# First weight batch of a spectral-mixing kernel: raw loads on GpSimd's queue, conversions in rounds

## The chip, the cores and the metric

The kernel runs on one core of a Trainium2 chip. The metric is the device time of one execution in microseconds (us), and each version is judged by the median of its runs. Engines are named as the profile names them: PE (TensorE), DVE (VectorE), ACT (ScalarE), POOL (GpSimd), and SP, the engine that issues most of the transfers. A transfer is issued on the queue of an engine and is carried by 16 DMA engines that all queues share.

## The reference

The reference filters a signal in the frequency domain along the sequence and passes the result through a two-layer block:

```python
# x: (8, 3008, 256) f32, filt_r, filt_i: (1505, 256) f32, w_in: (256, 2048) f64, w_out: (2048, 256) f64
X = np.fft.rfft(x, axis=1)
Y = X * (filt_r + 1j * filt_i)[None]
y = np.fft.irfft(Y, n=3008, axis=1).astype(np.float32).reshape(8 * 3008, 256)
h = y @ w_in
out = ((h - np.tanh(h)) @ w_out).astype(np.float32)
```

The weights come as 64-bit floats, which no engine computes with, so the kernel loads them as raw 64-bit words and builds 32-bit floats from their bits.

## The kernel before

**The transform.** The length 3008 is split as 64 x 47. For each batch there is a first stage (a matmul with `wf1` over the 64 points, whose results are stored to DRAM as `ct1`), a middle stage (read back as `a2`, one matmul with a matrix from `fg`, the product with the filter, a second pair of matmuls with `fg` and its turned copy `gx`, stored to DRAM as `ct2`), and a last stage (read back as `e2`, matmuls with `s2`, results in `ut`). Batches are worked off in units: batch 0 alone, then three pairs, then batch 7 alone.

**The two-layer block.** For every group of rows `up` makes h with Strassen-like products of `wu`, `shrink` computes h - tanh(h), and `down` multiplies with `wd`. `wu` and `wd` have seven strips: some come straight from the weights, the others are sums of strips, made on POOL by `sums`, four operations for each quarter of the columns. There are eight quarters: 0 to 3 for `wu`, 4 to 7 for `wd`. Both blocks run interleaved for all units, by an order that is written out by hand (`manual_schedule`): each engine executes its instructions in program order.

**The opening.** Before the interleaved loop begins, unit 0 goes through its first stage (`first0`, lines 853 to 876) and its 16 middle steps (the loop of line 966, j = 0 to 15, two steps to a group c of four matrices) with nothing beside them but the loading of weights. The change is confined to this opening.

- `converted` (line 191) handles one job, half a quarter: a 512 KB transfer into a tile `raw` (three buffers), three DVE operations that split the bits (lines 204 to 207), two operations for mantissa and exponent (ACT at lines 216 and 217, or DVE at 211 and 213 if `alone` is set), and four or five closing DVE operations (lines 219 to 230), the first of which reads `raw` for the last time.
- `weights_alone` (line 293) converts quarters 0 to 2 (six jobs) wholly on DVE during and after the first stage. `weights` (line 270) converts quarters 3 to 5 (six jobs), a round at each middle step. Both load `raw` on SP's queue. Quarters 6 and 7 follow in the main loop (`weights_slow`).
- At each even step the filters of the group after next are fetched by `filters_of` (line 878): six transfers on POOL's queue (ten for the last group). At each odd step `double_filters` (line 888, two ACT copies) prepares the filters of the next group and `turned` (line 895, two POOL operations) makes its `gx`.
- A middle step issues the loads for later groups on SP (`load_a2`, line 378; `load_slots`, line 370), the matmuls `pz`, then `back0` for the step before (line 951: matmuls `pe`, ACT copy to `e1s`, store to `ct2`), then the two filter products on DVE (lines 983 and 984), and then the weight round. "The gap" below is the time between the last middle step and the first matmuls `pu` of the last stage: the last store of `ct2` must land and be read back as `e2`.

Of the kernel before, what the change touches and what calls it, by code (L numbers as in the profile page):

```python
# [143 lines left out]
def kernel(  # L144
# [9 lines left out]
    nc = tc.nc  # L154
    V, G, ACT = nc.vector, nc.gpsimd, nc.scalar
# [35 lines left out]
    def converted(tiles, src, dsts, queue, alone=False):  # L191

        n = src.shape[-1] * (src.shape[1] if len(src.shape) == 3 else 1)
        t = tiles("raw", I64, n)
        queue.dma_start(t if len(src.shape) == 2 else
                        t.rearrange("p (h n) -> p h n", h=src.shape[1]), src)
        yield
        words = t.bitcast(I32).rearrange("p (n w) -> p n w", w=2)  # L200
        lo, hi = words[:, :, 0].bitcast(U32), words[:, :, 1]
        it, pt, st = (tiles(k, I32, n) for k in ("it", "pt", "st"))
        ft = tiles("ft", F32, n)
        V.tensor_scalar(out=it, in0=hi, scalar1=0xFFFFF, scalar2=None, op0=ALU.bitwise_and)
        V.tensor_scalar(out=pt, in0=hi, scalar1=20, scalar2=0x7FF,
                        op0=ALU.logical_shift_right, op1=ALU.bitwise_and)
        V.tensor_scalar(out=st, in0=hi, scalar1=-2 ** 31, scalar2=None, op0=ALU.bitwise_and)
        yield

        if alone:  # L210
            V.tensor_scalar(out=ft, in0=it, scalar1=2.0 ** -20, scalar2=1.0,
                            op0=ALU.mult, op1=ALU.add)
            V.tensor_scalar(out=pt, in0=pt, scalar1=-896.0, scalar2=0.0,
                            op0=ALU.add, op1=ALU.max)
        else:
            ACT.activation(ft, it, AF.Identity, bias=1.0, scale=2.0 ** -20)
            ACT.activation(pt, pt, AF.Relu, bias=exp_b)
        yield
        V.scalar_tensor_tensor(out=ft, in0=lo, scalar=2.0 ** -52, in1=ft,
                               op0=ALU.mult, op1=ALU.add)  # L220
        V.tensor_scalar_min(pt, pt, 255.0)
        yield
        V.scalar_tensor_tensor(out=pt, in0=pt, scalar=23, in1=st,
                               op0=ALU.logical_shift_left, op1=ALU.bitwise_or)
        pt = pt.bitcast(F32)
        for cols, dst, sign in dsts:
            f, p = ft[:, cols], pt[:, cols]
            if len(dst.shape) == 3:
                f, p = (v.rearrange("p (h n) -> p h n", h=dst.shape[1]) for v in (f, p))
            V.scalar_tensor_tensor(out=dst, in0=f, scalar=sign, in1=p, op0=ALU.mult, op1=ALU.mult)  # L230
        yield

    def parts_of(quarters):

        jobs = []
        for k in quarters:
            u = k % 4
            for h in range(2):
                if k < 4:
                    cols = slice(256 * u, 256 * u + 256)  # L240
                    src = bass.AP(tensor=moe_w_in.tensor, offset=128 * h * DFF + 256 * u,
                                  ap=[[DFF, 128], [DFF // 2, 2], [1, 256]])
# [12 lines left out]
        return jobs  # L255
# [6 lines left out]
        G.tensor_sub(w[:, 2], w[:, 1], w[:, 5])  # L262
        G.tensor_sub(w[:, 6], w[:, 0], w[:, 6])

    def begun(tiles, job, alone=False):
        j = converted(tiles, *job, nc.sync, alone)
        next(j)
        return j

    def weights(tiles, quarters, ahead):  # L270


        jobs = parts_of(quarters)
        began = [begun(tiles, job) for job in jobs[:ahead]]
        yield
        for k in range(len(jobs) + 1):
            if k < len(jobs):
                next(began[k])
            if k > 2 and k % 2:
                sums(quarters[k // 2 - 1])  # L280
            yield
            if k < len(jobs):
                next(began[k])
            if k > 0:
                for _ in began[k - 1]:
                    pass
            if k + ahead < len(jobs):
                began.append(begun(tiles, jobs[k + ahead]))
            yield
        sums(quarters[-1])  # L290
        yield

    def weights_alone(tiles, quarters):

        jobs = parts_of(quarters)
        began = [begun(tiles, job, True) for job in jobs[:2]]
        yield
        for k in range(len(jobs)):
            if k + 2 < len(jobs):
                began.append(begun(tiles, jobs[k + 2], True))  # L300
            for _ in began[k]:
                pass
            if k % 2:
                sums(quarters[k // 2])
            yield

    def weights_slow(tiles, quarters):

        jobs = parts_of(quarters)
        began = [begun(tiles, job) for job in jobs[:2]]  # L310
        yield
        for k in range(len(jobs)):
            for _ in began[k]:
                yield
            if k + 2 < len(jobs):
                began.append(begun(tiles, jobs[k + 2]))
            if k % 2:
                sums(quarters[k // 2])
                yield
# [511 lines left out]
    with tc.tile_pool(name="tr", bufs=2) as tr, tc.manual_schedule():  # L831
        with tc.tile_pool(name="pro", bufs=1) as pro, \
# [62 lines left out]
            def turned(g3, t):  # L895


                G.tensor_copy(t[0:RP], g3[IM:IM + RP])
                G.tensor_scalar_mul(t[IM:IM + RP], g3[0:RP], -1.0)
# [12 lines left out]
            V.memset(near_b, B)  # L912
            V.memset(exp_b, -896.0)
            xs = [load_x0(0, (0, 4, 8)), load_x0(1), load_x0(2)]
            ws = weights_alone(tiles0, range(3))

            pad = pro.tile([64, DM], F32, name="pad")
            G.memset(pad, 0.0)
# [12 lines left out]
            mats = {0: load_slots(0, pro)}  # L931
            next(ws)
            for c in range(3):
                for k, _ in enumerate(first0(xs[c], c)):
                    if k == 3:
                        next(ws)
            G.dma_start(s2, s2_d)
            turned(mats[0][1], gx[0])
            fts[1] = filters_of(1)
# [1 line left out]
            mats[1] = load_slots(1, pro)  # L941
            a2[1] = load_a2(0, 1, False, "ft")
            double_filters(fts[0], 0)
            for _ in ws:
                pass
            ws = weights(tiles0, range(3, 6), 2)
            next(ws)
            e1s = pro.tile([128, 4, 2, DM], F32, name="e1s")
            waiting = []

# [15 lines left out]
            for j in range(NK // 2):  # L966
                c = j // 2
                if j % 2 == 0 and c + 1 < NK // 4:
                    if c + 2 < NK // 4:
                        a2[c + 2] = load_a2(0, c + 2, False, ("a2", "ft")[c % 2])  # L970
                        mats[c + 2] = load_slots(c + 2, pro)
                        fts[c + 2] = filters_of(c + 2)
                pz = z0("pz", [128, 2, DM])
                for i in range(2):
                    k = (2 * j + i) % 4
                    nc.tensor.matmul(pz[:, i], mats[c][0][0:R2, k],
                                     a2[c][0:R2, k * DM:k * DM + DM], start=True, stop=True)
                if waiting:
                    back0()
                uv = tr.tile([128, 2, DM], F32, tag="uv", bufs=2, name="uv")  # L980
                zs = tr.tile([128, 2, DM], F32, tag="zs", bufs=2, name="zs")
                ft = fts[c][:, :, j % 2 * 2:j % 2 * 2 + 2]
                V.tensor_mul(uv, pz, ft[:, 0])
                V.tensor_mul(zs, pz, ft[:, 1])
                waiting.append((j, uv, zs))
                next(ws, None)
                if j % 2 and c + 1 < NK // 4:
                    double_filters(fts[c + 1], c + 1)
                    turned(mats[c + 1][1], gx[(c + 1) % 2])
                if j == NK // 2 - 3:  # L990
                    fs = first(1, z1)
                    next(fs)
                if j == NK // 2 - 1:
                    e2s[0] = load_e2(*groups[0], None, slice(0, 48))
            back0()
            for _ in range(EARLY):
                next(fs)
            load_e2(*groups[0], e2s[0], slice(48, 64))
            for _ in ws:
                pass  # L1000


        with tc.tile_pool(name="dn", bufs=2) as dn, \
# [40 lines left out]
            for U in range(total + 2):  # L1044
                i, u = divmod(U, 4)
                if U < total:
                    p, c = groups[i]
# [114 lines left out]
```

## Time and profile before

| what | value |
|---|---|
| median of 4 runs | 2839.16 us (2837.45 to 2841.6) |
| profiled execution, own time | 2838.55 us |
| its span, first to last instruction | 2836.7 us |
| mean granted PE clock | 0.988 |
| busy share of PE, DVE, ACT, POOL | 96%, 67%, 66%, 63% |
| first filter product of the middle stage (L983) | 52.51 us after the start |
| last filter product (L984) | starts at 112.36 us |
| first matmul of the last stage (L511) | 121.69 us |

The profile gives busy times, waits with the instruction or transfer that ended them, and stretches of the span. Times in it count from the start of the span. "L983" is line 983 of the kernel. A transfer's "issue" is the short time that it occupies its queue's engine; it lands later.

### The profile page before, as it was taken

Reading aid. Unit: us, or ns where it says so; the run is one execution under the profiler, and the core shown is the slowest. Engines: PE = TensorE matmul, PEld = TensorE weight load, DVE = VectorE, ACT = ScalarE, POOL = GpSimd, SP = SyncE. Lnnn points to the kernel's source line nnn. Section 1 sums busy time; section 2 is a strip of 40 time slices with the busy share of each in tenths; the row PEclk is TensorE's granted clock in tenths of the full one; section 3 lists DMA queues with packets and bytes.
Section 4 is the critical chain, followed back from the end, with each engine's and each line's share of the span. In section 5 each row is a group of like instructions: output and inputs, shape, how many; then the busy total and the mean of one; then the engine's idle time right before and its main releaser. Section 6 shows DMA issues by size and latency. Waiting matters only on the chain.

```text
span 2836.7 us, 36615 instructions
## 1 busy us (share of the span) xinstructions
PE 2728.6 (96%) x12418; PEld 2266.4 (80%) x12418; DVE 1913.9 (67%) x2170; ACT 1881.8 (66%) x2794; POOL 1793.4 (63%) x1407
## 2 busy tenths in 40 slices
PE   4799999999999999999999999999999999999998
PEld 2567777988877787888877787788888888898887
DVE  6565655666766677656666776676676767677776
ACT  2476766666767776666666667666676666666665
POOL 5456887544677767744577777755466667656555
PEclk7899999999999999999999999999999999999999
DMA  9754443232233332232332223212222322101010
GB/s 247 203 184 109 115 107 85 67 104 75 66 81 75 79 72 58 49 89 79 73 94 67 70 71 78 52 43 64 65 65 61 80 55 52 35 17 27 16 22 17
DMA packets 322592, 217.53 MB, mean 77 GB/s; under 512 B 224782, under 2 KB 274746, under 8 KB 322156
## 3 DMA queue, kind: packets, MB, share of 16 engines
q1 hardware_dynamic: 266826, 157.28, 23.7%
q10 hardware_dynamic: 52818, 51.53, 6.0%
q0 software_dynamic: 2752, 6.30, 0.8%
q8 instruction: 100, 1.64, 0.2%
q14 instruction: 96, 0.79, 0.1%
HBM read 138.87 MB, written 79.17 MB: 77 GB/s over the span
## 4 chain that ended last, share of the span: by engine, by line
PE 77%; ACT 9%; issue 5%; DVE 4%; DMA 3%; POOL 1%; ACTq 1%; DVEq 0%; SPq 0%; POOLq 0%
PE o L653 31%; PE x L545 20%; PE z L545 9%; PE y L545 5%; PE pe L411 3%; PE pu L511 3%; ACT y L601 3%; PE pz L430 3%; PE pf L351 2%; DVE h L607 1%; ACT u L551 1%; ACT zs L444 1%; ACT y L602 1%; DVE uv L445 1%; ACT zs L443 1%
## 5 line engine op out<-in xcount | busy, mean ns | idle before, releaser
L653 PE MATMUL o<-t,wd 128*128 128x256 f32 (+2 forms) x3072 | 774.8, 375 | 1.8 <-POOL t L526 1.3
L607 DVE TENSOR_TENSOR h<-h,y 128x1024 f32<-128x1024 f32 (+2 forms) x384 | 571.8, 1489 | 279.7 <-ACT y L602 279.7
L653 PEld LDWEIGHTS o<-t,wd 128*128 128x128 f32 x3072 | 579.3, 190 | 73.8 <-POOL t L526 1.6
L545 PE MATMUL x<-tu,wu 128*128 128x256 f32 (+2 forms) x2304 | 588.8, 378 | 15.4 <-ACT u L551 15.1
L653 PE MATMUL o<-h,wd 128*128 128x256 f32 (+2 forms) x2304 | 581.5, 375 | 0.2 <-DVE h L611 0.2
L611 DVE SCALAR_TENSOR_TENSOR h<-sq,h 128x1024 f32<-128x1024 f32 (+2 forms) x384 | 567.0, 1477 | 20.5 <-ACT y L601 0.5
L524 POOL TENSOR_TENSOR t<-h 128x512 f32<-128x512 f32 (+2 forms) x192 | 240.3, 1252 | 502.4 <-DVE h L611 444.7
L545 PEld LDWEIGHTS x<-tu,wu 128*128 128x128 f32 x2304 | 427.8, 190 | 159.1 <-issue 73.1
L653 PEld LDWEIGHTS o<-h,wd 128*128 128x128 f32 x2304 | 430.7, 190 | 71.2 <-issue 18.8
L608 ACT ACTIVATE sq<-y,near_b 128x1024 f32<-128x1024 f32 (+2 forms) x384 | 435.6, 1134 | 5.0 <-DVE h L611 0.2
L601 ACT ACTIVATE y<-h 128x1024 f32<-128x1024 f32 (+2 forms) x384 | 400.0, 1042 | 14.8 <-ACT e L414 8.0
L602 ACT ACTIVATE y<-y 128x1024 f32<-128x1024 f32 (+2 forms) x384 | 399.2, 1040 | 12.1
L551 ACT COPY s<-x 128x512 f32<-128x512 f32 (+2 forms) x192 | 110.9, 577 | 443.3 <-PE x L545 434.7
L527 POOL TENSOR_TENSOR t<-t,h 128x512 f32<-128x512 f32 (+2 forms) x192 | 307.6, 1602 | 0.1
L551 ACT COPY u<-x 128x512 f32<-128x512 f32 (+2 forms) x384 | 219.3, 571 | 55.5 <-PE x L545 20.0
L525 POOL TENSOR_TENSOR t<-h,t 128x512 f32<-128x512 f32 (+2 forms) x192 | 241.2, 1256 | 15.1
L526 POOL TENSOR_TENSOR t<-h 128x512 f32<-128x512 f32 (+2 forms) x191 | 248.1, 1299 | 0.0
L575 DVE TENSOR_TENSOR h<-z,u 128x512 f32<-128x512 f32 (+2 forms) x192 | 129.5, 675 | 171.3 <-ACT u L551 168.4
L446 POOL TENSOR_TENSOR zs<-zs,ft 128x512 f32<-128x512 f32 x112 | 166.0, 1483 | 101.9 <-ACT zs L444 101.8
L447 POOL TENSOR_TENSOR uv<-uv,zs 128x512 f32<-128x512 f32 x112 | 213.8, 1909 | 14.0 <-DVE uv L445 5.5
L545 PE MATMUL x<-ut,wu 128*128 128x256 f32 (+2 forms) x768 | 199.3, 382 | 4.8 <-DVE h L581 3.0
L561 DVE TENSOR_TENSOR h<-y,s 128x512 f32<-128x512 f32 (+2 forms) x192 | 130.4, 679 | 104.9 <-PE y L545 87.5
(119 smaller groups left out, 3384.7 us busy)
## 6 DMA issues: line engine op xcount, KB each, us to landing
a<-ct SPq DMA_DIRECT2D x64, 384.0 KB, 4.1
ft<-filt SPq DMA_DIRECT2D x96, 256.0 KB, 4.5
out_dram<-ot SPq DMA_DIRECT2D x1392, 16.0 KB, 1.5
ct<-e ACTq DMA_DIRECT2D x112, 192.0 KB, 2.6
ct<-a ACTq DMA_DIRECT2D x80, 256.0 KB, 2.9
x_sb<-in_x_dram SPq DMA_DIRECT2D x69, 256.0 KB, 2.8
e<-ct SPq DMA_DIRECT2D x33, 512.0 KB, 4.4
fg<-fg SPq DMA_DIRECT2D x40, 392.0 KB, 6.4
```

The lines of the kernel that those rows point to most:

```text
L524: G.tensor_sub(t[0], b[0][1], b[0][0])
L525: G.tensor_sub(t[1], b[1][1], t[0])
L526: (V if shared else G).tensor_sub(t[2], b[1][1], b[0][1])
L527: G.tensor_sub(t[3], t[1], b[1][0])
L545: nc.tensor.matmul(bank[:, k], wu[:, q - 1, (2 * u + k) * 128:(2 * u + k + 1) * 128], rhs[q - 1], start=(first and k == 0), stop=True, ski ...
L551: ACT.copy(t, X)
L601: ACT.activation(y[k], ht[k], AF.Arctan, scale=S)
L602: ACT.activation(y[k], y[k], AF.Square, accum_out=y_sums[:, 2 * U + k // 2:2 * U + k // 2 + 1])
L607: V.tensor_mul(ht[k], ht[k], y[k])
L608: ACT.activation(sq[k], y[k], AF.Square, bias=near_b, scale=A)
L611: V.scalar_tensor_tensor(out=ht[k], in0=sq[k], scalar=K, in1=ht[k], op0=ALU.add, op1=ALU.mult)
L653: nc.tensor.matmul(product(q), wd[:, q - 1, (2 * u + k) * 128: (2 * u + k + 1) * 128], rhs[q - 1][:, k], start=(u == 0 and k == 0 and q == ...
```

## The change

- `weights` takes over quarters 0 to 4 (ten jobs), in rounds, with its two middle operations on ACT. `weights_alone` is gone. Quarter 5 (two jobs) is a generator of its own.
- All twelve raw loads of the opening go to POOL's queue (`G`).
- Two raw loads are issued before the first stage, none within it. Behind the first stage come five rounds: all but the end of jobs 0 and 1, and the first three operations of job 2. Each middle step has one round, and at odd steps it now stands behind `double_filters` and `turned`. So jobs 2 to 9 fall into the middle steps (the end of job 9 behind them).
- The raw loads of quarter 5 are issued at step 13; its conversion and its sums stand in the gap, with those of quarter 4.

```diff
-    def weights(tiles, quarters, ahead):
+    def weights(tiles, quarters):
         jobs = parts_of(quarters)
-        began = [begun(tiles, job) for job in jobs[:ahead]]
+        began = [begun(tiles, job, G) for job in jobs[:2]]
         yield
         for k in range(len(jobs) + 1):
             if k < len(jobs):
                 next(began[k])
...
             if k > 0:
                 for _ in began[k - 1]:
                     pass
-            if k + ahead < len(jobs):
-                began.append(begun(tiles, jobs[k + ahead]))
+            if k + 2 < len(jobs):
+                began.append(begun(tiles, jobs[k + 2], G))
             yield
...
-    def weights_alone(tiles, quarters):
...
-            ws = weights_alone(tiles0, range(3))
+            ws = weights(tiles0, range(5))
...
             for c in range(3):
-                for k, _ in enumerate(first0(xs[c], c)):
-                    if k == 3:
-                        next(ws)
+                for _ in first0(xs[c], c):
+                    pass
...
             double_filters(fts[0], 0)
-            for _ in ws:
-                pass
-            ws = weights(tiles0, range(3, 6), 2)
-            next(ws)
+            for _ in range(5):
+                next(ws)
...
                 waiting.append((j, uv, zs))
-                next(ws, None)
                 if j % 2 and c + 1 < NK // 4:
                     double_filters(fts[c + 1], c + 1)
                     turned(mats[c + 1][1], gx[(c + 1) % 2])
+                next(ws)
                 if j == NK // 2 - 3:
                     fs = first(1, z1)
                     next(fs)
+                    ws_gap = weights(tiles0, range(5, 6))
+                    next(ws_gap)
...
             load_e2(*groups[0], e2s[0], slice(48, 64))
-            for _ in ws:
-                pass
+            for w in (ws, ws_gap):
+                for _ in w:
+                    pass
```

More of the change, by code (lines that the diff above doesn't have):

```diff
@@ L263, in sums, with begun @@
         G.tensor_sub(w[:, 6], w[:, 0], w[:, 6])
-    def begun(tiles, job, alone=False):
-        j = converted(tiles, *job, nc.sync, alone)
+    def begun(tiles, job, queue, alone=False):
+        j = converted(tiles, *job, queue, alone)
         next(j)
         return j
-    def weights(tiles, quarters, ahead):
+    def weights(tiles, quarters):
         jobs = parts_of(quarters)
-        began = [begun(tiles, job) for job in jobs[:ahead]]
+        began = [begun(tiles, job, G) for job in jobs[:2]]
         yield
@@ L291, in weights @@
         yield
-    def weights_alone(tiles, quarters):
[L295 to L301, printed above, removed]
-                pass
-            if k % 2:
-                sums(quarters[k // 2])
-            yield
     def weights_slow(tiles, quarters):
         jobs = parts_of(quarters)
-        began = [begun(tiles, job) for job in jobs[:2]]
+        began = [begun(tiles, job, nc.sync) for job in jobs[:2]]
         yield
@@ L315, in weights_slow @@
             if k + 2 < len(jobs):
-                began.append(begun(tiles, jobs[k + 2]))
+                began.append(begun(tiles, jobs[k + 2], nc.sync))
             if k % 2:
@@ L998 @@
             load_e2(*groups[0], e2s[0], slice(48, 64))
-            for _ in ws:
-                pass
+            for w in (ws, ws_gap):
+                for _ in w:
+                    pass
         with tc.tile_pool(name="dn", bufs=2) as dn, \
```

## The prediction, on record before the result

> **What bounds the kernel now.** The page first. Behind the first slice PE is busy nine tenths to the end, so a change to the opening is worth what the opening gets shorter; in the first four slices (71 us each) the DMA engines are fullest.
>
> ```profile
> PE   4799999999999999999999999999999999999998
> DMA  9754443232233332232332223212222322101010
> ```
>
> Second, the stages as windows: busy us (count) of PE, PEld, DVE, ACT, POOL, then granted clock, DMA share and GB/s.
>
> ```profile
> 0.00:37.60 37.60, 13.89 (x26) 4.92 (x26) 15.51 (x34) 10.12 (x16) 17.74 (x30) 0.85 0.92 262
> 37.60:52.50 14.90, 3.75 (x8) 2.52 (x8) 13.82 (x29) 0.00 (x0) 5.62 (x8) 0.50 0.99 258
> 52.50:109.80 57.30, 42.78 (x161) 29.84 (x162) 44.62 (x81) 27.72 (x38) 48.76 (x71) 0.87 0.88 212
> 109.80:121.70 11.90, 7.15 (x30) 4.54 (x28) 2.58 (x4) 4.11 (x7) 0.00 (x0) 1.00 0.55 154
> ```
>
> From 37.6 to 52.5 DVE is full and ACT idle: DVE converts weights while the first filter product waits. From 52.5 to 109.8 POOL is the fullest. Third, DVE's timeline at the seam, then POOL's near the end.
>
> ```profile
> 51.84 0.76 DVE L230 SCALAR_TENSOR_TENSOR wu<-conv 128x256 f32<-128x256 f32 x2
> 52.51 0.68 DVE L983 TENSOR_TENSOR uv<-pz,filt 128x512 f32<-128x512 f32 x1
> ```
> ```profile
> 84.15 0.76 POOL L885 DMA_DIRECT2D filt<-in_filt_r_dram  x1
> 84.90 0.55 POOL L885 DMA_DIRECT2D filt<-in_filt_i_dram  x1
> ...
> 89.71 0.60 POOL L885 DMA_DIRECT2D filt<-in_filt_r_dram  x1
> 90.30 0.55 POOL L885 DMA_DIRECT2D filt<-in_filt_i_dram  x1
> 93.13 0.56 POOL L885 DMA_DIRECT2D filt<-in_filt_r_dram  x1 [2.27 <-DMA filt<-in_filt_r_dram]
> 94.86 0.54 POOL L885 DMA_DIRECT2D filt<-in_filt_i_dram  x1 [1.17 <-DMA filt<-in_filt_i_dram]
> ...
> 99.16 0.72 POOL L260 TENSOR_TENSOR wd<-wd 128x256 f32<-128x256 f32 x1
> ...
> 103.67 1.24 POOL L899 TENSOR_SCALAR gx<-fg 48x384 f32<-48x384 f32 x1
> ```
>
> L983 starts the moment the conversions end. The issue at 93.13 is the eighth behind the one at 84.15 and waited for a landing, and so did 94.86 behind 84.90: I read that POOL's ninth transfer waits until the first has landed. The sums (99.16) stand ahead of the turned copy (103.67), for which PE waits until 104.96. From 52.68 to 109.79 POOL worked without a break but for such landings (6.4 us in five waits). So three things bound the opening: DVE at its start, POOL with its landings in its middle, DMA close behind both.
>
> **The first stage.** Five raw loads run beside it now; then three and the next group's filters: 2560 - 1536 - 376 = 648 KB less, at 262 GB/s 2.5 us. The bounds are 0 (the raw loads now stand in a third queue beside the stores) and 4 us; I take 2. The load of `a` (L382), issued at 37.64, goes at 35.6.
>
> **The first product.** PE's first pz began at 42.48, 4.84 behind that issue; its four matmuls take about 1.9, so the product could start at 44.4 and starts at 52.51: 8.1 us stand in DVE's queue. DVE then has only job 0, three operations each of jobs 1 and 2: 3.6 + 1.0 + 1.0 us (L204 to L230 without contention), beside the first stage's tail. First product: 42.4, 10 us earlier. If raw load 2 lands late, all of this is lost; it is issued near 26 and landings of raw loads took 9.8 us in the median, 16.2 at most, so the cover is real.
>
> **The middle steps.** Six jobs lay in them, now nearly eight, still one job to two steps, with their middle operations on ACT as before; a pair of steps costs DVE 2 x 1.2 + 3.6 = 6.0 us, ACT about 5.2. Raw loads 4 to 9 are issued here by POOL, so SP no longer holds `a` and `fg` behind them; that I cost at nothing, for PE waited for `a` once (9.5 us, at the start). POOL gains an issue of about 0.7 us per pair (its issues took 0.51 to 0.76). The raw issue waits for the job's L219 on DVE, and behind it on POOL stand `turned`, sums and filters. The walk, with 3.45 us for six filter issues, 1.75 for a turned copy, 3.2 for sums: raw 4 at 43.6 (product, then L219), turned and sums to 49.25, filters 3 to 52.7, raw and turned to 55.15. Filters 4 now meet the ninth-transfer rule: a raw load makes seven transfers per pair, so each waits for the one issued just one pair and one issue before. What a landing takes there is the disputed size. Filters landed in 6.7 us in the median and 10.0 at most from 50 to 110; with the raw loads ahead of them in their queue I take 8.0, and 0.3 to release. Then filters 4 go on at 57.55 and end at 60.4; with raw, turned and sums filters 5 start at 66.05, end at 69.5; filters 6 go on at 74.35, end at 77.2; sums to 82.85; filters 7 start at 83.15, their ninth at 91.45; raw 9 at 92.6; turned 6 ends at 95.05 (104.9 before: the sums no longer stand ahead of it). Raw 9 lands at 100.6, its three operations end at 101.6, and behind them on DVE waits the product of step 14 (110.08 before). From there to the end of the last pe took 5.0 us (115.06); the closing four operations of job 8, 2.55 us, now stand between the last two products, of which 0.3 is hidden: 7.25. The stage ends at 108.85, 6.2 us earlier. One us more of landing counts at four places (filters 4, 6, 7, raw 9) and costs 4 us.
>
> **The gap.** DVE gets the end of job 9 and jobs 10 and 11: 2.55 + 2 x 3.6 = 9.75 us, behind its last product; ACT their four operations (2.6 us), ahead of the `ut` copies; POOL two sums (6.4 us), ahead of the combination for `tu` (L524). By rows: the last sums end about 13 us behind the last pe, L524 and L525 1.4 later, and the matmul that reads `tu` stood 15 us behind it (130.01). So it is covered by half a us to a us; contention of DVE and POOL (L205 took 0.95 instead of 0.42 beside sums) may cost 0 to 4 us. I take 1. A raw load 11 landing over 6 us behind the last pe would stop ACT and so `ut`; it is issued 3 us before.
>
> **Sum.** -6.2 + 1 = -5.2 us on the profiled execution, whose own time was 2838.55 for a span of 2836.7 and lies 0.6 under the median: 2834.0 for the median. Nothing behind the opening changes place.
>
> **A rule against it.** From 37.6 to 52.5 the DMA engines were at 0.99 and 258 GB/s with the queues as they are. The Trainium skill, DMA: Bandwidth & Descriptors, Rules for kernel authors, says that spreading transfers over SP, ACT and GpSimd gains no bandwidth, as all run on the same engines. By it alone only the 2 us of the first stage and DVE's reordering would count, as here. The same page (Anatomy of one DMA) would give a 512 KB load 2.0 us plus size over 436 GB/s, 3.2 us as an estimate; the rows' 9.8 us contradict that under load, and by 3.2 us no landing would bind and the next case would follow.
>
> **Rivals.** (1) *The early start comes through.* Landings stay at the 6.7 us of now: 1.3 us less at four places ends the stage at 103.65, net -10.4, 2828.8. For it: SP's loads no longer wait for raw buffers, the DMA share from 52.5 to 109.8 is only 0.88. A floor is near: 14.5 MB between the load of `a` and raw 9 take 56 us at 258 GB/s, until 92. (2) *Slower: the ninth transfer.* Raw loads put 512 KB beside 376 KB of filters into one queue; if landings rise past 9.3 us, four waits eat the gain (114.1), and at 11 us the stage ends at 120.9, net +6.8, 2846. For it: landings up to 10.0, 16.2 for raw loads. Against: median 6.7. (3) *The move cancels*: POOL's chain, not DVE, sets the end at the same place, within 3 us of 2839; landings of 9 us do that.
>
> **How the numbers follow.** Forecast 0.40 (its own range 2830 to 2838: landings of 7 to 9 us, 4 us of time for each), rival 1 0.28, rival 2 0.20, rival 3 0.12. 0.2% is 5.7 us, about what a measurement can tell: faster than 2833.5 is rival 1 and less than half of the forecast (0.18), 0.46; slower than 2844.8 is rival 2, 0.20; between, 0.34. The range 2827 to 2846 leaves out the far ends.
>
> **What would show it.** L983 first at about 42; ACT copies (L216) for ten jobs before the gap; POOL waiting for raw and filter landings in the middle, 4 to 8 us in all; PE's pe ending near 109; `tu` (L524) within 2 us of its old distance. Wrong if L983 starts past 48, if DVE's L204 waits for raw loads by over 10 us, or if L524 waits for sums by over 3.

## The result, and the profile after

The changed kernel takes 2836.38 us in the median of 40 runs (2833.29 to 2839.31); the kernel before took 2839.95 in the median of 60 runs beside it (2834.83 to 2843.95). The ratio is 0.9987, 95% interval 0.9982 to 0.9991: 3.6 us faster, or 0.13%. The forecast was 2834.0, in the range 2827 to 2846. The profiled execution took 2835.7 us for a span of 2833.9; before it was 2838.55 for 2836.7.

Lines of `converted`, `sums` and `begun` (191 to 268) keep their numbers. Most lines behind `weights` stand 13 lower than before (`pu` L498, `ut` L500, `tu` L511 to L514, the filter loads L872, the doubled filters L876 and L877, the turned copies L885 and L886). From `back0` through the middle loop they stand 16 lower (the `pe` matmuls L941 and L943, the filter products L967 and L968).

The page's busy tenths, one digit for 71 us: a tenth more for PE in the first slice and nothing else for PE; the DMA engines differ by a tenth in three slices.

```profile
PE   5799999999999999999999999999999999999998
DMA  9754443233233322222332223212222322101010
```

The same four stages, and then the third one's first 47.5 us in two parts (busy us and count of PE, PEld, DVE, ACT, POOL; granted clock, DMA share, GB/s):

```profile
0.00:37.60 37.60, 14.52 (x26) 5.69 (x26) 5.02 (x14) 12.53 (x20) 20.85 (x35) 0.85 0.88 256
37.60:52.50 14.90, 11.79 (x41) 8.25 (x42) 11.35 (x21) 5.74 (x8) 11.29 (x17) 0.80 1.05 240
52.50:109.80 57.30, 42.93 (x157) 28.08 (x155) 46.02 (x86) 28.71 (x39) 42.71 (x63) 0.88 0.86 231
109.80:121.70 11.90, 4.95 (x19) 4.51 (x20) 10.06 (x20) 4.13 (x7) 5.91 (x8) 0.58 0.84 238
52.50:80.00 27.50, 19.70 (x76) 13.22 (x75) 19.72 (x38) 13.82 (x19) 20.32 (x31) 0.88 1.03 275
80.00:100.00 20.00, 14.17 (x52) 9.29 (x51) 17.40 (x31) 9.58 (x14) 19.08 (x28) 0.87 0.74 196
```

The second stage now does middle steps: ACT has 5.74 us of work there where it had none, PE 11.79 instead of 3.75. From 37.6 to 80 us the DMA engines are full, and from 80 to 100 POOL is busy for 19 of 20 us. The gap (109.8 to 121.7) holds 10 us of DVE's work instead of 2.6. DVE at the seam, then DVE and POOL near the end of the middle:

```profile
41.10 0.69 DVE L967 TENSOR_TENSOR uv<-pz,filt 128x512 f32<-128x512 f32 x1 [2.43 <-issue]
42.30 0.68 DVE L219 SCALAR_TENSOR_TENSOR conv<-raw,conv 128x512 f32<-128x512 uint32 x1
...
98.18 0.43 DVE L204 TENSOR_SCALAR conv<-raw 128x512 int32<-128x512 int32 x1 [2.46 <-DMA raw<-in_moe_w_out_dram]
...
100.73 0.69 DVE L967 TENSOR_TENSOR uv<-pz,filt 128x512 f32<-128x512 f32 x1 [0.39 <-ACT filt L876]
```
```profile
92.93 0.76 POOL L197 DMA_DIRECT2D raw<-in_moe_w_out_dram  x1
...
96.18 1.16 POOL L886 TENSOR_SCALAR gx<-fg 48x384 f32<-48x384 f32 x1
97.42 0.72 POOL L260 TENSOR_TENSOR wu<-wu 128x256 f32<-128x256 f32 x1
```

The first filter product starts at 41.10 instead of 52.51 and stands ahead of L219. The turned copy (96.18) is now ahead of the sums (97.42). The raw load of 92.93 holds DVE until 98.18, and the product of step 14 follows at 100.73 (110.08 before). The last `pe` ends at 107.80 instead of 115.22.

Marks of all kernels, from their traces, in us from the span's start. "Closing" is the start of the last of the 384 closing products of `shrink` (L598; L611 before); "main loop" is the way from `x<-tu`, the first matmul of `up` that reads `tu`, to it.

| kernel | `a` issued | first product | last `pe` ends | first `ut` copy | `x<-tu` | closing | main loop | span | median |
|---|---|---|---|---|---|---|---|---|---|
| before | 37.64 | 52.51 | 115.22 | 123.46 | 130.01 | 2816.79 | 2686.8 | 2836.7 | 2839.95 |
| before, second profile | 37.85 | 52.48 | 115.96 | 124.48 | 131.21 | 2818.10 | 2686.9 | 2837.8 | |
| after | 34.89 | 41.10 | 107.80 | 118.16 | 123.89 | 2812.80 | 2688.9 | 2833.9 | 2836.38 |
| after, second profile | 34.89 | 41.07 | 107.61 | 117.97 | 123.93 | 2813.26 | 2689.3 | 2832.9 | 2836.00 |
| SP's queue | 35.09 | 45.02 | 106.27 | 116.62 | 122.38 | 2810.11 | 2687.7 | 2831.5 | 2833.28 |
| old place | 34.94 | 41.22 | 106.06 | 116.42 | 122.91 | 2812.22 | 2689.3 | 2833.7 | 2835.58 |
| both of these | 33.81 | 43.85 | 106.96 | 117.32 | 123.68 | 2813.10 | 2689.4 | 2834.9 | 2836.99 |
| no gap | 34.97 | 41.21 | 107.41 | 115.77 | 121.39 | 2815.95 | 2694.6 | 2837.6 | 2839.69 |
| queue alone | 36.37 | 57.18 | 121.49 | 129.84 | 135.48 | 2823.45 | 2688.0 | 2845.3 | 2849.76 |
| one slot load | 35.56 | 41.64 | 102.25 | 112.61 | 118.59 | 2805.99 | 2687.4 | 2829.1 | 2832.07 |
| filters on SP | 40.10 | 46.35 | 116.26 | 126.61 | 133.47 | 2823.36 | 2689.9 | 2844.7 | 2844.85 |
| sums behind | 35.62 | 45.63 | 108.17 | 118.53 | 125.49 | 2814.91 | 2689.4 | 2837.1 | 2837.48 |
| gap in other tiles | 35.26 | 45.25 | 106.62 | 115.13 | 121.85 | 2811.59 | 2689.7 | 2833.4 | 2833.16 |
| delay | 35.86 | 42.22 | 108.99 | 119.35 | 128.49 | 2818.40 | 2689.9 | 2839.2 | 2839.29 |

### The profile page after: what moved, and what is told of

The parts are those of the page before. It is cut to its first block, busy times and chain, and to the rows that moved or that the text cites. A ratio compares the mean times of both kernels' runs of the same rounds, so it can differ in the third digit from the quotient of the medians.

```text
span 2833.9 us, 36616 instructions
## 1 busy us (share of the span) xinstructions
PE 2732.0 (96%) x12418; PEld 2272.7 (80%) x12418; DVE 1907.5 (67%) x2158; ACT 1889.0 (67%) x2806; POOL 1801.8 (64%) x1419
## 4 chain that ended last, share of the span: by engine, by line
PE 77%; ACT 9%; issue 5%; DVE 4%; DMA 2%; POOL 2%; ACTq 1%; SPq 0%; DVEq 0%; POOLq 0%
PE o L640 31%; PE x L532 20%; PE z L532 9%; PE y L532 5%; PE pe L398 3%; PE pu L498 3%; ACT y L588 3%; PE pz L417 3%; PE pf L338 2%; DVE h L594 1%; ACT u L538 1%; ACT zs L431 1%; ACT y L589 1%; DVE uv L432 1%; ACT zs L430 1%
## 5 line engine op out<-in xcount | busy, mean ns | idle before, releaser
L598 DVE SCALAR_TENSOR_TENSOR h<-sq,h 128x1024 f32<-128x1024 f32 (+2 forms) x384 | 566.7, 1476 | 20.8 <-DVE h L594 0.5
L511 POOL TENSOR_TENSOR t<-h 128x512 f32<-128x512 f32 (+2 forms) x192 | 240.4, 1252 | 500.2 <-DVE h L598 448.5
L514 POOL TENSOR_TENSOR t<-t,h 128x512 f32<-128x512 f32 (+2 forms) x192 | 307.0, 1599 | 0.1
L512 POOL TENSOR_TENSOR t<-h,t 128x512 f32<-128x512 f32 (+2 forms) x192 | 241.1, 1256 | 15.1
```

The lines of the kernel that those rows point to most:

```text
L511: G.tensor_sub(t[0], b[0][1], b[0][0])
L512: G.tensor_sub(t[1], b[1][1], t[0])
L514: G.tensor_sub(t[3], t[1], b[1][0])
L598: V.scalar_tensor_tensor(out=ht[k], in0=sq[k], scalar=K, in1=ht[k], op0=ALU.add, op1=ALU.mult)
```

## The experiments

Two questions: which part of the change brings the gain, and why 7.4 us at the last `pe` are 3.6 at the end. Each ratio is to runs of the kernel before taken beside the experiment (medians of 2838.71 to 2839.59 us).

**1. The raw loads back on SP's queue.** In the changed kernel:

```diff
-        began = [begun(tiles, job, G) for job in jobs[:2]]
+        began = [begun(tiles, job, nc.sync) for job in jobs[:2]]
...
-                began.append(begun(tiles, jobs[k + 2], G))
+                began.append(begun(tiles, jobs[k + 2], nc.sync))
```

> The changed kernel with its raw loads back on SP's queue; rounds, order and gap stay. Theory A (the gain is the reordering of the conversions; the queue is incidental): first filter product within 1 us of 41.1, last pe within 2 us of 107.8, median within 1.5 us of the changed kernel. Theory B (the gain is the queue: SP no longer holds the loads of a and fg behind raw buffers): last pe back at 112 to 115, median within 1 us of the kernel before.

2833.28 us, ratio 0.9982 (0.9973 to 0.9991). The first product comes 4 us later, as DVE waits 5.9 us for a raw load ahead of it, and the last `pe` 1.5 us earlier than in the changed kernel. Theory A holds for the last `pe`, but its first product is 3 us off and the median lies 3.1 us below the changed kernel's instead of within 1.5. Theory B's numbers did not come: POOL's queue is not what brings the gain.

**2. The round of conversions at its old place**, ahead of `double_filters` and `turned`:

```diff
                 waiting.append((j, uv, zs))
+                next(ws)
                 if j % 2 and c + 1 < NK // 4:
...
-                next(ws)
```

> The changed kernel with the weight round of a middle step ahead of double_filters and turned again, as before. Theory A (POOL's chain ends the middle; sums ahead of the turned copy delay PE): sums stand ahead of turned at four odd steps, PE waits 3 us for gx at two or three of them, last pe 109.5 to 112, median 1 to 3 us above the changed kernel. Rival (the order only shifts waiting between engines): last pe within 1 us of 107.8, no difference.

2835.58 us, ratio 0.9986 (0.9977 to 0.9995); last `pe` at 106.06, 1.7 us earlier than in the changed kernel, where the rival allowed 1 and theory A wanted it later. No gain of the new place is to be seen, so the prediction's credit for it (the turned copy ahead of the sums) was not on the path any more.

**3. No quarter in the gap**: quarter 5 is converted in the main loop.

```diff
-                    ws_gap = weights(tiles0, range(5, 6))
-                    next(ws_gap)
...
-            for w in (ws, ws_gap):
-                for _ in w:
-                    pass
+            for _ in ws:
+                pass
...
-            late, copies = weights_slow(tiles1, range(6, 8)), filters_d()
+            late, copies = weights_slow(tiles1, range(5, 8)), filters_d()
```

> The changed kernel with quarter 5 taken out of the gap and converted in the main loop, in front of quarters 6 and 7. Theory C (the gap is not free: the first ut copy waits until the last conversion there has released its tiles, and tu waits for the sums): the first ut copy stands 8.4 us behind the last pe instead of 10.4, the first matmul that reads tu 15.0 instead of 16.1, median 1 us below the changed kernel, if the main loop takes the two jobs without loss. Rival (the gap is covered, as DVE has nothing else there): no difference at the ut copy; then the two jobs in the main loop can only cost, 0 to 3 us.

2839.69 us, ratio 1.0002 (0.9993 to 1.0011). `x<-tu` stands 13.98 us behind the last `pe` instead of 16.09: the quarter costs the gap 2.1 us, twice what theory C had there. But in the main loop it costs more: that is 2694.6 us long, 5.7 more than in the changed kernel, and the median is 3.3 us above it, just past the rival's 0 to 3.

**4. The queue alone**: the kernel before, with its opening's raw loads on POOL's queue and nothing else of the change.

```diff
-    def begun(tiles, job, alone=False):
-        j = converted(tiles, *job, nc.sync, alone)
+    def begun(tiles, job, alone=False, queue=G):
+        j = converted(tiles, *job, queue, alone)
...
-        began = [begun(tiles, job) for job in jobs[:2]]
+        began = [begun(tiles, job, False, nc.sync) for job in jobs[:2]]
...
-                began.append(begun(tiles, jobs[k + 2]))
+                began.append(begun(tiles, jobs[k + 2], False, nc.sync))
```

The last two pairs are in `weights_slow`, the main loop's, which so keeps SP's queue.

> The kernel before with the raw loads of its opening on GpSimd's queue, nothing else changed. Theory A: the first product stays at 50 to 54, POOL gains 0.7 us of issue per pair of steps and its ninth-transfer waits grow, last pe 114 to 119, median 0 to 4 us above the kernel before. Theory B: SP runs ahead, last pe 109 to 112, median 3 us below the kernel before.

2849.76 us, ratio 1.0039 (1.0026 to 1.0053): 10 us slower. Both theories missed: the first product comes at 57.18, later than either had it, and the last `pe` ends at 121.49. POOL's timeline of this kernel (its lines are those of before):

```profile
57.34 0.72 POOL L260 TENSOR_TENSOR wu<-wu 128x256 f32<-128x256 f32 x1 [12.80 <-DVE wu L230]
...
60.30 0.73 POOL L197 DMA_DIRECT2D raw<-in_moe_w_in_dram  x1
```

The sums wait 12.8 us for DVE's conversion (L230), and the next raw load stands behind them on POOL, while DVE waits for raw loads twice (6.1 us until 53.04, just behind a landing at 52.96, and 6.6 until 65.10). One thing hangs on the next: DVE needs the load, the load stands behind the sums, the sums need DVE. In the changed kernel's rounds the sums stand a job behind the conversion that they need, and from 34 to 110 us POOL waits for L230 once, 4.7 us, at the start of the gap.

**5. One load of the middle's slots.** The changed kernel without seven of its eight `fg` loads, so that it computes with the first slots throughout:

```diff
-            mats[1] = load_slots(1, pro)
+            mats[1] = mats[0]
...
-                        mats[c + 2] = load_slots(c + 2, pro)
+                        mats[c + 2] = mats[0]
```

> The changed kernel, with the middle step's slots (fg) loaded once instead of eight times: the computation leaves out seven of the eight fg loads (about 2.7 MB) and uses the first slots for all. Theory A (bytes: from 37.6 to 80 us the changed kernel's DMA share is 1.03 to 1.05, so the middle waits for what the queues can carry): 2.7 MB at the 275 GB/s of that window are some 10 us, so raw's landings become shorter, the DVE's waits for raw (11.0 us in five) fall under 4 us, and the last pe ends at 98 to 103 instead of 107.8; the time is 4 to 9 us below the changed kernel's 2836. Theory B (GpSimd: from 80 to 100 us it is busy 19 of 20 us with filter issues, turned and sums): last pe stays at 106 to 109, and so does the time.

2832.07 us, ratio 0.9975 (0.9965 to 0.9985); last `pe` at 102.25, as theory A had it. The same two windows as the last two of the changed kernel:

```profile
52.50:80.00 27.50, 23.57 (x97) 15.20 (x96) 26.40 (x48) 17.76 (x25) 26.51 (x39) 1.00 0.84 247
80.00:100.00 20.00, 15.40 (x47) 10.42 (x46) 15.40 (x30) 8.85 (x13) 16.08 (x24) 0.74 0.51 145
```

Fewer bytes, and DVE works 26.4 us instead of 19.7 in the first of them, POOL 26.5 instead of 20.3; DVE's waits for raw in the middle fall from 11.0 to 3.6 us. The raw loads issued from 43 to 69 us land in 6.2 to 7.6 us, where the changed kernel's took up to 13.6. The middle, from the first product to the last `pe`, takes 60.6 us instead of 66.7, and in the changed kernel no wait of PE, DVE, ACT or POOL in the middle ended at an `fg` load. So bytes hold some 6 us of it; behind them DVE and POOL, full from 52.5 to 80, are next.

**6. The filters' loads on SP's queue.** In the changed kernel:

```diff
-                    G.dma_start(t[IM * v + row:IM * v + row + m, v, i:i + n], src)
+                    nc.sync.dma_start(t[IM * v + row:IM * v + row + m, v, i:i + n], src)
```

> The changed kernel, with the filters' loads (filters_of) issued by SyncE instead of by GpSimd; nothing else. Theory A (bytes bound the middle): the same bytes, so last pe ends at 106 to 109 and the time is within 1.5 us of the changed kernel's. Theory B (GpSimd's work bounds the middle): GpSimd loses some 0.75 us for each filter load, over 10 us between 40 and 100 us, so last pe ends at 101 to 104, and the time is 3 to 5 us below the changed kernel's. A third outcome, last pe later than 110, would say that loads behind a filter load that waits for its tile on SyncE are what is late.

2844.85 us, ratio 1.0016 (1.0007 to 1.0025). The third outcome came: the load of `a` goes at 40.10, behind the filters, and ACT waits for filters. From the waits of this kernel from 34 to 110 us (engine, line, what ended the wait; total, times, longest):

```profile
ACT filt L876 <- DMA filt<-in_filt_r_dram: 15.4, 4, 6.3
```

Even without the late start the middle takes 69.9 us instead of 66.7, with POOL busy 13.5 instead of 20.3 us from 52.5 to 80. Relieving POOL bought nothing in this form. How much it would buy with the filters in time, this run can't say.

**7. Both undone**: SP's queue and the old place together (the edits of 1 and 2).

> The changed kernel with the raw weights back on SyncE's queue and the round of conversions back ahead of the doubling and turning (the place it had before): only the rounds, their five quarters ahead, and the quarter in the gap are left of the change. Theory: the gain comes from these alone. The two undone parts each measured 0.9982 and 0.9986 of the kernel before alone, so neither gives anything: last pe at 104.5 to 107 and 2832 to 2836 us (ratio 0.997 to 0.9985). Rival: the two undone parts were needed by each other, or one of them by the reordering, and the time rises above 2837.

2836.99 us, ratio 0.9992 (0.9983 to 1.0001); last `pe` at 106.96 as expected, the time 1 us above the expected range and just short of the rival's, and not clear of the kernel before. Its opening is level with the changed kernel's (`x<-tu` 123.68 against 123.89), so the rounds and the five quarters ahead are what shortens the opening; by the time alone that is not shown.

**8. The gap's last sums behind `last`.** In the kernel of 7:

```diff
-            for w in (ws, ws_gap):
-                for _ in w:
-                    pass
+            for _ in ws:
+                pass
+            for _ in range(6):
+                next(ws_gap)
...
             for _ in last(0, z1):
                 pass
+            next(ws_gap)
```

> As the kernel with the raw weights on SyncE's queue and the old place of the round, and with the last four sums of the quarter in the gap issued behind the second group's differences of the first batch (last) instead of ahead of them. Theory (the gap's price of some 2 us is the four sums on GpSimd that tu's subtractions stand behind): tu starts right behind the ut copies, x<-tu 1 to 2 us closer to the last pe, 1 to 2 us less than the kernel without this edit. Rival (the price is the ut copy that waits for the quarter's last conversion, since its tile takes over that memory): x<-tu stays at E + 15.5 to 17 and the time is the same within 0.7 us.

2837.48 us, ratio 0.9993 (0.9984 to 1.0002). `tu` now follows the `ut` copy at once, at 119.19, and `x<-tu` still stands 17.3 us behind the last `pe` (16.7 in 7). That is 0.3 us beyond the rival's range and far from the theory's, and the times are 0.5 us apart. The sums are not the gap's price; the rival holds.

**9. The gap's quarter through other tiles.** In the kernel of 1, with the edit of 8. `tiles1`, which hands out the main loop's tiles (the pool `tr`), is defined ahead of it:

```diff
-                    ws_gap = weights(tiles0, range(5, 6))
+                    ws_gap = weights(tiles1, range(5, 6))
```

> As the kernel with the raw weights back on SyncE's queue (and the changed place of the round), with two edits in the gap: its quarter is converted through the tiles that the main loop's conversions use (tr) instead of through the opening's memory (pro), which the first ut tile takes over; and its last four sums stand behind the second group's differences (last). Theory (the gap costs 2.1 us because the first ut copy waits for the last reader of that memory): the first ut copy starts 8.2 to 8.8 us behind the last pe, as before the change, instead of 10.4, x<-tu at most 15.2 us behind it, and the time is 1 to 2.5 us below the kernel that only has SyncE's queue (2833.3, ratio 0.9982), so ratio 0.997 to 0.9978. Rival (the copy waits for something else, or the raw transfer into a later tile delays the gap's conversions): ut stays at 10 us or more and the time at 2833 or above.

2833.16 us, ratio 0.9979 (0.9970 to 0.9988). ACT and DVE in the gap, of the changed kernel and then of this one:

```profile
117.10 0.83 DVE L230 SCALAR_TENSOR_TENSOR wd<-conv 128x256 f32<-128x256 f32 x3
118.16 0.58 ACT L500 COPY ut<-pu 128x512 f32<-128x512 f32 x1 [4.86 <-DMA e<-ct]
```
```profile
115.13 0.58 ACT L500 COPY ut<-pu 128x512 f32<-128x512 f32 x1 [3.02 <-PE pu L498]
115.92 1.29 DVE L230 SCALAR_TENSOR_TENSOR wd<-ft,pt 128x256 f32<-128x256 f32 x3
```

In the changed kernel the copy starts 0.23 us behind the end of the last conversion (117.93) and 10.36 us behind the last `pe`. The releaser named there had long been done. With the conversions in other tiles the copy goes ahead of them, 8.51 us behind the last `pe` (8.24 before the change). That settles why the copy was late: the first `ut` tile takes over memory of the opening's tiles, and so waited for their last reader. The time is not below that of 1, as the theory wanted. Of the 1.8 us at the copy, 0.9 are left at `x<-tu` (15.23 us behind the last `pe` against 16.11): the granted clock was one half until 120.93 us, so that the matmuls `y<-ut` ahead of it took 1.81 us, where those of 1, at 120.66 and behind the clock's return at 120.46, took 1.03. `x<-tu` leads that kernel's by 0.5 us only, and the main loop is 2 us longer.

**10. The changed kernel again.**

> The changed kernel, unchanged, in a second profile. Theory (which of the half-clock stretches of 3.41 us a run gets is a property of its instructions' distances): the stretches stand again at 248 us for 6.83 us and 5.7 us behind the last closing product, the closing product 383 starts within 0.3 us of 2812.8. Rival (they fall by the execution): at least one of the stretches is missing, shorter or elsewhere, and the closing product 383 is 0.5 to 3 us off 2812.8 with the same times up to 130 us within 0.3 us.

2836.0 us, ratio 0.9990 (0.9980 to 1.0001). The half-clock stretch of 6.83 us at 248 us stands there again; the one behind the last closing product is gone, and the way from that product to the end takes 19.6 us instead of 21.1. The last closing product is 0.46 us off 2812.8, between the theory's 0.3 and the rival's 0.5. As far as two executions can tell, the former stretch goes with the kernel and the latter with the execution.

**11. A pure delay behind the opening.** In the changed kernel:

```diff
-            ACT.copy(ut[:, h, 0:n], pu[:, 0:n])
+            for _ in range(5 if (i, h) == (0, 0) else 1):
+                ACT.copy(ut[:, h, 0:n], pu[:, 0:n])
```

> The changed kernel with the first copy of ut made five times instead of once: a pure delay of about 2.3 us on the chain between the opening and the main loop, and no other difference. If a microsecond of the opening is worth a microsecond at the end, x<-tu comes at 126.0 to 126.5 and the time is 2 to 2.5 us above the changed kernel's (2838 to 2839). If the main loop's own losses (half-clock stretches, products of DVE and GpSimd that meet) decide what remains of a shift, the end moves by less than 1 us or more than 4, and the lead of the closing products changes in jumps at about 250 and about 490 us, as it does between the kernels so far.

2839.29 us, ratio 1.0000 (0.9991 to 1.0009), 2.9 above the changed kernel. Neither outcome is clean: its middle ended 1.2 us later by itself and `x<-tu` came at 128.49, 4.6 later instead of 2.3. The lead over the kernel before, 1.5 us, held at 250 us (1.45 before and behind it) and fell to -1.2 at 500 us, with a half-clock stretch at 492.7. So here a shift does not come through whole: it loses or gains in jumps at these two places.

**12. The kernel before again.**

> The kernel before, unchanged, in a second profile. In its first profile the main loop from x<-tu to the closing product 383 took 2686.8 us, the shortest of all kernels here (the others 2687.4 to 2689.9 where the main loop's instructions are the same), and the tail behind that product 19.9 us. Theory (the main loop's length is a property of the kernel, by where the opening's end falls against the half-clock stretches): 2686.5 to 2687.1 us again, with one stretch of 3.41 us at 255 us and none at 490. Rival (the first profile was a lucky execution): 2688 to 2690 us, with a stretch near 490 us or a collision there, which would give back 1 to 3 us of the opening's lead of 6.1.

One run, 2839.62 us. The main loop took 2686.9 us again, with one stretch of 3.41 us at 256.6 us and none at 490. In the two profiles of each of these kernels the length goes with the kernel, not with the execution. But the 60 runs of the kernel before lie up to 9.1 us apart, and where they differ no trace shows.

## Why the prediction was right, and where it was not

**The first stage.** Forecast: `a` issued 2 us earlier. Measured: 2.75 us (34.89 against 37.64). That is inside its bounds of 0 to 4 us.

**The first product.** Forecast 42.4, measured 41.10. The conversions that stood ahead of it are gone, and raw load 2 was in time.

**The middle's end.** Forecast: last `pe` at 108.85. Measured: 107.80 and 107.61. (For the end before, the walk took 115.06, the start of the matmul behind it; it is 115.22.) The number held, in part by luck. The walk was right in the order of POOL's queue: raw load 4 issued at 43.28 (forecast 43.6), raw load 9 at 92.93 (92.6), step 14's product at 100.73 (101.6), 7.07 us from there to the end of `pe` (7.25). It was right too that POOL would wait for landings, 4 to 8 us in all:

```profile
57.33 0.64 POOL L872 DMA_DIRECT2D filt<-in_filt_r_dram  x1 [1.45 <-DVE conv L204]
58.64 0.53 POOL L872 DMA_DIRECT2D filt<-in_filt_i_dram  x1 [0.67 <-DVE uv L967]
...
76.24 0.64 POOL L872 DMA_DIRECT2D filt<-in_filt_r_dram  x1 [1.10 <-ACT filt L876]
77.92 0.53 POOL L872 DMA_DIRECT2D filt<-in_filt_i_dram  x1 [1.04 <-ACT e1s L946]
```

The names in the brackets mislead. The issue of 57.33 is the eighth behind the raw load of 43.28, which landed at 56.74; that of 76.24 is the eighth behind the raw load of 63.42, landed at 75.65. The two others are the eighth behind filter loads that landed at 58.05 and 77.33. Each goes on 0.59 us behind that landing. It did not need the DVE and ACT work named: the loads overwrite the filters of the group before, whose last products had ended at 54.65 and 74.45. In the trace POOL's transfers take eight semaphores in turn, and an issue waits for the last transfer on its own semaphore. That makes the ninth-transfer rule that the prediction read off; whether the chip has such a limit besides, no run here tells. Counted by landings, POOL waited 6.9 us in eleven places, of which the names give 1.8 to filter loads.

What failed inside the walk is its one landing time of 8.0 us. The raw loads issued from 36 to 63 us took 11.6 to 13.6 us to land, while the DMA engines were full (a share of 1.05 and 1.03); those of 72.59, 80.67 and 92.93 took 7.8, 6.9 and 5.2. So filters 4 and 6 waited longer than forecast, filters 7 not at all, and raw load 9 landed sooner. That these errors cancelled is luck. And DVE waited for raw loads not only at raw load 9, as the walk had it, but five times, as the waits of the changed kernel from 34 to 110 us say:

```profile
DVE conv L204 <- DMA raw<-in_moe_w_in_dram: 8.6, 4, 4.2
DVE conv L204 <- DMA raw<-in_moe_w_out_dram: 2.5, 1, 2.5
```

11 us, just past the 10 us that the prediction had named as a sign that it was wrong. In experiment 1 these waits are 2.0 us behind the first product, and yet the last `pe` ends only 1.5 us earlier: waits show where time went, not what taking them away would bring.

The floor of bytes that the prediction set beside rival 1 fits what was measured. From the load of `a` (34.89) to raw load 9 (92.93) the transfers moved 14.2 MB in 58.0 us, at 244 GB/s; the floor was 14.5 MB in 56 us. SP, no longer held by raw loads, issued seven loads of `a` and `fg` between 34.9 and 38 us; how much of the long landings is due to that no run separates. With fewer bytes (experiment 5) the landings fell to the 6.7 us of rival 1 (6.2 to 7.6), POOL waited for none in the middle, and the stage ended at 102.25, near that rival's 103.65. By that experiment it is the bytes that kept **rival 1**, the early start, from coming through.

**Rival 2**, the ninth transfer, did not come: landings passed its 9.3 us in the first half of the middle, but not in the second. **Rival 3** put the time within 3 us of 2839, and 2836.38 lies there too; but by its mechanism the stage would have ended at the same place, and it ended 7.4 us earlier. Half of the opening's gain is gone at the end through two other things than POOL's chain.

**The gap.** Forecast +1, from the sums ahead of `tu`. Measured +2.1 against the kernel without the quarter (3), and +1.2 as a mean of two profiles against the kernel before (16.2 us from the last `pe` to `x<-tu` against 15.0). The size was near; the mechanism was wrong. `tu` started 13.4 us behind the last `pe` instead of 8.9, outside the 2 us that the prediction allowed, 2.5 us behind the end of its first `ut` copy and right behind the sums. But the part of `tu` that `x<-tu` reads (L512) had ended at 122.74, 1.15 us before `x<-tu`, and taking the sums away (8) moved nothing. The `ut` copy itself was late, through the shared memory (9), and with it the matmuls up to `x<-tu`; in 9 that is 0.9 us of the price, and the rest was not taken apart. A trace of before could not show that; the tile pools in the code could.

**"Nothing behind the opening changes place."** This is the step that failed, and it cost 2.1 to 2.4 us. By the means of two profiles each, the lead is 7.9 us at the last `pe`, 6.7 at `x<-tu`, 4.4 at the last closing product and 3.9 at the end; the medians say 3.6. The main loop has the same instructions, and it takes 2686.8 and 2686.9 us before and 2688.9 and 2689.3 after. Two places carry it. In the first profiles the lead of the closing products is 6.5 us at 165 us, 5.1 at 267 us, 4.2 at 499 us and 4.0 at the last one (times of the kernel before). The first place, in windows of the kernel before and then of the changed one, the latter 7 us earlier:

```profile
253.00:259.00 6.00, 3.39 (x7) 2.04 (x8) 4.76 (x4) 3.24 (x5) 5.84 (x4) 0.72 1.04 247
259.00:265.00 6.00, 6.00 (x28) 4.87 (x27) 1.13 (x2) 5.06 (x8) 2.12 (x2) 1.00 0.77 198
```
```profile
246.00:252.00 6.00, 3.19 (x6) 1.72 (x6) 4.92 (x4) 3.66 (x5) 5.84 (x5) 0.69 1.00 246
252.00:258.00 6.00, 6.00 (x20) 4.58 (x20) 0.25 (x1) 3.19 (x5) 1.38 (x1) 0.74 0.93 233
```

PE pauses in both kernels (some 3.3 of 6 us busy), and the clock falls to one half. Before it is back for the next 6 us (1.00); after it stays low for half of them (0.74), 6.83 us in all instead of 3.41. That costs 1.5 us. The kernel of experiment 1 missed this stretch and gained 1.5 us there instead; it has one at 486 us, where its lead falls by 2.7. The Trainium skill, TensorE: Matmul & The Clock Gate, Part 1, says that the gate looks at activity in free-running windows of 3.41 us. The 3.41 and 6.83 us agree. It also says that the phase varies from run to run; here the stretch at 248 us came in both profiles of the changed kernel, and only the one in the tail came and went.

The second place, DVE and POOL beside each other, of the kernel before and then of the changed one:

```profile
491.30 1.09 DVE L611 SCALAR_TENSOR_TENSOR h<-sq,h 128x896 f32<-128x896 f32 x1
...
491.50 2.03 POOL L446 TENSOR_TENSOR zs<-zs,ft 128x512 f32<-128x512 f32 x1 [1.25 <-ACT zs L444]
```
```profile
486.18 2.05 DVE L598 SCALAR_TENSOR_TENSOR h<-sq,h 128x896 f32<-128x896 f32 x1
...
486.00 1.27 POOL L433 TENSOR_TENSOR zs<-zs,ft 128x512 f32<-128x512 f32 x1 [0.88 <-ACT zs L431]
```

Two products meet. Before, DVE comes first by 0.20 us, and POOL's product takes 2.03 us instead of 1.27. After, POOL comes first by 0.18, and DVE's takes 2.05 instead of 1.09. In each case the later one ends 0.13 us before the time at which it would have, had it started when the first was done. After: 486.00 + 1.27 + 1.09 = 488.36, measured 488.23. Before: 491.30 + 1.09 + 1.27 = 493.66, measured 493.53. DVE's is on the path: its next product followed at 492.31 before and at 488.14 after, so the lead falls by 0.95 us here. The Trainium skill, SBUF — State Buffer, SBUF: two separate sides, has the rule: the two engines share a pair of ports as an exclusive lock for a whole instruction, and the later one blocks. These rows agree.

**The rule on queues**, which the prediction took from the Trainium skill (DMA: Bandwidth & Descriptors, Rules for kernel authors), agrees with the rows: nothing was gained by the third queue. The rate from 37.6 to 52.5 is 240 GB/s after and was 258 before, and experiment 1 gives all of the gain without it.

**The sum.** -7.4 at the last `pe` (forecast -6.2), +1.3 in the gap (+1), +2.1 in the main loop (0), +1.2 in the tail (0) give the 2.8 us between the first two spans. The second profile of the changed kernel lacks the tail's 1.2. The time came inside the range and on the forecast's side, 2.4 us above it. The middle's extra 1.2 us hid part of the 3.3 us that the sum had at nothing. Of the prediction's three chances the change fell within 0.2%, which had 0.34, and not beyond, which had 0.46. A term for the main loop, of both signs and about 2 us, was missing from the range's working.

**Better versions.** The kernels of experiments 1 and 9 have the lowest times of those that compute all (ratios 0.9982 and 0.9979). Their intervals overlap with the changed kernel's, so that they beat it is not shown; that they beat the kernel before is.

## What to carry to other kernels

Moving work out of one engine's queue at a stage's start pays there until the next shared resource, here the bytes in flight, sets the stage's end; count the bytes from the new start to the end before crediting the earlier start. A wait put down to an engine whose work was not needed is to be checked against the landings of the transfers before it. Tiles that a new stage takes over from an old one carry hidden waits, so look at what last reads that memory before work is moved to the end of a stage. A shift of a few us ahead of a long loop arrives only within the loop's own jumps (half-clock stretches, engines that meet), so give it a term of that size and of both signs.

## What the runs showed that was not expected

- The queue of a transfer is worth 10 us by what stands ahead of it: raw loads behind POOL's sums wait for DVE, which waits for the raw loads (experiment 4).
- Half-clock stretches of PE in the main loop came in 3.41, 6.83 and 10.24 us, multiples of one length; two profiles of the changed kernel shared those in the main loop but not that in the tail.
- The one that comes second waits: 0.2 us of difference in start decided whether DVE's product took 2.05 us instead of 1.09 or POOL's 2.03 instead of 1.27.
- A 512 KB load landed in 13.6 us (issued at 53.32, with a DMA share of 1.03 from 52.5 to 80) or in 5.2 us (issued at 92.93, share 0.74 from 80 to 100) in the same stage.
- Eleven waits of POOL's transfers, 6.9 us in all, ended at the landing of the transfer eight issues earlier; the profile puts four of them down to an instruction of DVE or ACT, three to nothing, and four to the landing.
